# Forgetting attention and a bilinear feed-forward on one core: reciprocals of the softmax sums as powers on GpSimd, from the third batch on

## The chip, the cores and the metric

The kernel runs on one core of a Trainium2 chip. The metric is the device time of one execution in microseconds (us); lower is better. Engines go by the names of the profile: PE (TensorE matmuls), PEld (its weight loads), DVE (VectorE), ACT (ScalarE), POOL (GpSimd), SP (SyncE, which here only issues DMAs).

## The reference

Attention with a forget gate, over 8 batches, 8 heads, 576 positions and a head size of 64, is followed by a bilinear feed-forward over the 4608 tokens of 512 features:

```python
scores = scale * np.matmul(q, k.transpose(0, 1, 3, 2))
cum = np.cumsum(np.log(np.clip(f, 0.0001, 1.0)), axis=-1)
scores = np.where(causal, -1e9, scores + cum[:, :, :, None] - cum[:, :, None, :])
attn = np.exp(scores - np.max(scores, axis=-1, keepdims=True))
attn = attn / (np.sum(attn, axis=-1, keepdims=True) + 1e-09)
x = np.matmul(attn, v)                  # then heads side by side: 4608 x 512
out = ((x @ w_a) * (x @ w_b)) @ w_out   # d_ff = 1536
```

The division by the row's sum is what the change is about.

## The kernel before

The unit of attention is a pair of heads of one batch, numbered t from 0 to 31 (four pairs a batch). Its 576 query rows are five blocks i: four of 128 rows, for which both heads are worked on one after the other, and a last one, i = 4, with 64 rows of each head side by side on the 128 partitions. For each block, in this order:

- PE multiplies q and k into PSUM (`qk_first`, `qk_group`; tiles sc). From the third batch on a POOL copy (`last_queries`, L610, tile qd) first lays out the last 64 queries.
- DVE adds the decay from the tile spread to the scores, writes them to S, and takes the row's maximum in the same instruction (`do_decay`, L673, one for each head). In the first batch a plain maximum is taken instead (L645). The causal mask lies in spread; POOL makes it there (`mask_copy`, L630, and `mask_last`, L637).
- ACT takes the exponential into the tile PA (blocks 0 to 2) or PB (blocks 3 and 4) and sums the rows as it goes (`do_exp`, L700 and L704). In the profile each shows as an ACTIVATE and an ACTIVATION_READ_ACCUMULATOR, which writes the sum.
- DVE takes the reciprocal of the sums (`do_recip`, L712 for block 4 with one column, L714 for the others with two columns, one for each head).
- POOL multiplies PA or PB by the reciprocals (`do_norm`, L725, one instruction for each head). In the first two batches ACT may do some of these (L723); from the third batch on POOL does all.
- A DMA from SP transposes PA and PB into PTA and PTB (`do_tr`, L739), PE multiplies these by v (`do_pv_all`, L768 and L783, tile pvx), and ACT or DVE copies the result to xT.

The maxima, sums and reciprocals of a head pair lie in one small tile st of 128 x 32 values: sums from column 10 (18 for block 4), reciprocals from column 20 (28 for block 4).

POOL has other work in between: it converts q, k and v to 16 bit (L290, L292), and issues some loads. The feed-forward runs beside the attention of later batches: PE's products psa and psb (all in L74), a copy of psa by ACT (L288), the product ht by DVE (L1072), PE's pso, and a copy and a store. The last 1024 tokens go through a scheme with fewer products (wg, wb), where POOL and DVE combine tiles in L1273.

Nothing is scheduled when the program is built: every step is an `Op` with a number, the list ORDER gives all 2463 numbers in one sequence, and each step is emitted to its engine as the sequence comes to it. So an engine's queue is that sequence with the other engines' steps left out. CHOICE gives the engine of those steps that have more than one. Each engine works through its queue strictly in turn; waits on other engines are semaphores that the framework puts in.

`EARLY` is (0, 1), the first two batches; `NP`, the head pairs of a batch, is 4.

Of the kernel before, what the change touches and what calls it, by code (L numbers as in the profile page):

```python
# [9 lines left out]
FP32 = mybir.dt.float32  # L10
# [15 lines left out]
def kernel(  # L26
# [11 lines left out]
    nc = tc.nc  # L38
# [7 lines left out]
    NP = H // 2  # L46
# [3 lines left out]
    def pool(name, bufs=1, **kw):  # L50
        return ctx.enter_context(tc.tile_pool(name=name, bufs=bufs, **kw))

    perm = pool("perm")
# [18 lines left out]
    def mm_halves(out, lhsT, rhs, **kw):  # L72
        for r in HP:
            nc.tensor.matmul(out=out[r], lhsT=lhsT[:, r], rhs=rhs, **kw)  # L74

    def identity():
        make_identity(nc, ident16)

    def wake(n):
        x = ff_tile([128, 512], FP32, "wake")  # L80
        for _ in range(n):
            mm_halves(x, ident16, ident16[:, 0:1].to_broadcast([128, 512]), start=True, stop=True, skip_group_check=True)
# [22 lines left out]
    def paddings():  # L105
        for x in (*qd, lowd):
            nc.gpsimd.memset(x, 0.0)
        for r in HP:
            nc.gpsimd.tensor_copy(out=lowd[r, r], in_=low[0][r, 0:64])
        for x in PB:  # L110
            nc.gpsimd.memset(x[:, 12, 64:128], 0.0)
        for i in range(2):
            nc.gpsimd.memset(nv[i][64:128, NSB - 1, :, :], 0.0)

# [74 lines left out]
    def take(op, tag):  # L189

        users = [op]
        op.takes.append((tag, users))
        return users
# [53 lines left out]
    for n in range(24):  # L247
        o = Op("PE", 0.427, lambda _: wake(2), [o_i], prio=-290, mode="full", name=f"wake{n}")
# [7 lines left out]
    for lo, hi in ((0, 256), (256, S)):  # L256
# [3 lines left out]
            out=cw["l"][FR, lo:hi], in_=cw["f"][FR, lo:hi], func=LN), [o1, o_w], prio=-300, name="fln")  # L260
        o3 = Op("DVE", 0.02 + 0.00232 * n, lambda _, lo=lo, hi=hi: scan(lo, hi), [o2, o0] + ([o3] if lo else []),
                prio=-300, name="fscan")
        o4 = Op("DVE", 0.06 + 0.0007 * n, lambda _, lo=lo, hi=hi: nc.vector.tensor_copy(
            out=crow[FR, lo:hi], in_=cw["f"][FR, lo:hi]), [o3], prio=-300, name="fhi")
# [8 lines left out]
    for u in s_users:  # L273
        u.extend([o_f[1], o6])
    o_p = Op("POOL", 4.0, lambda _: paddings(), [o_c], prio=-100)


# [106 lines left out]
    EARLY = tuple(range(2))  # L384
# [255 lines left out]
    def do_max(t, i):  # L640
        if ("st", t) not in T:
            T[("st", t)] = slot(st_pool, [128, 32], FP32, "st", "st")
        st = T[("st", t)]
        m = st[:, 8:9] if i == 4 else st[:, 2 * i:2 * i + 2]
        nc.vector.tensor_reduce(out=m, in_=T[("s", t, i)], axis=AXX, op=MAX, negate=True)  # L645
# [31 lines left out]
    def part_of(t, i):  # L677

        if i >= 3:
            return "B"  # L680
        return ("A0" if i < 2 else "A1") if t // NP in EARLY else "A"
# [26 lines left out]

    def do_recip(t, i):
        st = T[("st", t)]  # L710
        if i == 4:
            nc.vector.reciprocal(out=st[:, 28:29], in_=st[:, 18:19])  # L712
        else:
            nc.vector.reciprocal(out=st[:, 20 + 2 * i:22 + 2 * i], in_=st[:, 10 + 2 * i:12 + 2 * i])  # L714

    def do_norm(e, t, i, h):
        st = T[("st", t)]
        if i == 4:
            p, c = p_blocks(t, 4), 28
        else:  # L720
            p, c = p_blocks(t, i)[:, :, h, :], 20 + 2 * i + h
        if e == "ACT":
            nc.scalar.activation(out=p, in_=p, func=COPY, scale=st[:, c:c + 1])  # L723
            return
        VEC[e].tensor_scalar(out=p, in0=p, scalar1=st[:, c:c + 1], scalar2=1.0, op0=MUL, op1=MUL)  # L725
# [87 lines left out]
    def in_turn(o, kind, n, started=False):  # L813

        if (kind, n) not in first_of:
            first_of[(kind, n)] = o
            p = first_of.get((kind, n - 1))
            if p is not None:
                (o.prev if started else o.deps).append(p)

    def attention(t, base):
        b, pr = divmod(t, NP)

        def prio(g):
            if b == 0:
                return -100 + (3.0 * pr if g == 0 else 20 + 8 * pr + g)
            if b in EARLY:
                return base - 10 * pr + (3.0 * pr if g == 0 else 12 + 7 * pr + g)
            return base + g
# [30 lines left out]
        for gs in ([(0,), (1,), (2, 3)] if b in EARLY else [(0, 1), (2,), (3,)]):  # L860
# [5 lines left out]
            def stage(_, gs=gs):  # L866
# [3 lines left out]
                for g in gs:  # L870
# [3 lines left out]
                    prio=prio(gs[0]), mode="full" if full else "row", name=f"qk{t}.{gs[0]}")  # L874
            if full:
                cp = Op("POOL", 0.4, lambda _: last_queries(t), [kq_ops[("q", b, pr)], o_p] + last_qd[-1:], prio=prio(0),
                        name=f"qd{t}")
# [20 lines left out]
        for g, gi in [(g, groups[g]) for g in ((0, 1, 3, 2) if t in MASKP else (0, 1, 2, 3))]:  # L898
            qk, su = qk_of[g], None
            for i in gi:  # L900
                sc = users_of[i]
                part = part_of(t, i)
                mxs = []
                for h in range(1 if direct else 2):
                    fn = (lambda _, i=i: do_max(t, i)) if direct else lambda _, g=g, i=i, h=h: do_decay(t, g, i, h)
                    mx = Op("DVE", (MAXD if direct else RED)[i], fn,
                            [qk] if direct else [qk, bcs[h] if t not in MASKP or i == 4 else ml if i == 3 else mc], prio=prio(g),
                            name=f"max{t}.{i}")
                    if t in MASKP and i == 4:
                        ml.deps.append(mx)  # L910
                    in_turn(mx, "max" + part[0], t)
                    if st_users is None:
                        st_users = take(mx, "st")
                    else:
                        mx.deps.append(st_users[0])
                        st_users.append(mx)
                    if direct:
                        su = sc
                    else:
                        if su is None:  # L920
                            su = take(mx, "S")
                        else:
                            mx.deps.append(su[0])
                            su.append(mx)
                        bcu.append(mx)
                    (sc[h] if isinstance(sc, tuple) else sc).append(mx)
                    mxs.append(mx)
                    if direct:
                        for x in direct_ex.get(g, []):
                            x.deps.append(mx)  # L930
                es = []
                for h in range(1 if i == 4 else 2):
                    ex = Op("ACT", EXPD[i], lambda _, i=i, h=h: do_exp(t, i, h),
                            mxs if i == 4 or direct else mxs[h:h + 1], prio=prio(g),
                            name=f"exp{t}.{i}")
                    if direct:
                        ex.deps.append(o_e)
                        direct_ex.setdefault(g, []).append(ex)
                    ex.tail = 0.005
                    in_turn(ex, "exp" + part[0], t)  # L940
                    if part not in pu:
                        if part == "A1":
                            ex.deps.append(pu["A0"][0])
                            pu["A0"].append(ex)
                            pu[part] = pu["A0"]
                        else:
                            pu[part] = take(ex, "P" + part[0])
                        if part == "B":
                            ex.deps.extend([o_p] + last_pb[-1:])
                            last_pb.append(ex)  # L950
                    else:
                        ex.deps.append(pu[part][0])
                        pu[part].append(ex)
                    es.append(ex)
                su.extend(es)
                rc = Op("DVE", 0.16, lambda _, i=i: do_recip(t, i), es, prio=prio(g))
                st_users.extend(es + [rc])
                for h in range(1 if i == 4 else 2):
                    nm = Op(None, {"POOL": NORM[i]} | ({"ACT": 0.2 + 0.00082 * 128 * (i + 1)} if b in EARLY else {}), lambda e, i=i, h=h: do_norm(e, t, i, h), [rc], prio=prio(g),
                            name=f"norm{t}.{i}")  # L960
                    st_users.append(nm)
                    pu[part].append(nm)
                    norms.setdefault(part, []).append(nm)
                    norm_of.append((i, nm))
        trs, ptu = {}, {}
        la_users = None
        for part in norms:
            lo, hi = BLOCKS[part]
            p = prio({"A0": 0, "A1": 1}.get(part, 2))
            if b in PEP or (t, part) in PEQ:  # L970
                cuts = {"A": [(0, 6), (6, 12)], "A0": [(0, 6)], "A1": [(6, 12)], "B": [(0, 8), (8, 13)]}[part]
                trs[part] = []
                for lo, hi in cuts:
# [7 lines left out]
                            prio=p - 0.5, name=f"pev{t}{part}")  # L981
# [46 lines left out]
        for rows in [(0, 1), (2, 3)]:  # L1028
# [5 lines left out]
                    prio=p, mode="col", name=f"pv{t}")  # L1034
            pvu = take(pv, "ff")
            ev = Op("DVE", 0.15 + 0.00106 * 128 * len(rows), lambda e, rows=rows: do_ev(e, t, rows), [pv], prio=p - 1,
                    name=f"ev{t}")
# [319 lines left out]
    for b in range(B):  # L1357
        batch_inputs(b, 40.0 * b + (-100.0 if b == 0 else 0.0))
        if b == 0:
            weights(-85.0)  # L1360
        for pr in range(NP):
            attention(b * NP + pr, 40.0 * b + 10.0 * pr + 30)
# [168 lines left out]
```

## Time and profile before

| | |
|---|---|
| median of 2 runs (lowest to highest) | 396.73 us (396.17 to 397.29) |
| the profiled execution, its own time | 395.96 us |
| its span, first to last instruction | 393.9 us |
| busy: PE, DVE, ACT, POOL | 382.3, 319.2, 296.5, 280.4 us |
| L725 on POOL, scaling of PA (180) and of PB (90) | 85.6 and 64.0 us |
| L673 on DVE, decay and maximum, the form with 232 | 125.4 us |
| L704 on ACT, exponential, PA (168) and PB (56) | 84.1 and 40.2 us |

In the profile's groups a row reads: line, engine, operation, the tile written and those read with their shapes, the count; then busy time in all and the mean ns of one; then how long the engine stood idle just before such instructions, and which engine's instruction ended most of that. In the timeline a row is: start, length, engine, line, operation, tiles; an x2 at its end says that two like instructions were merged, and brackets give the idle time ahead with what ended it. A group of waits reads: who waited, for whom, us in all, how often, and the longest. All times are from the start of the span.

### The profile page before, as it was taken

Reading aid. Unit: us, or ns where it says so; the run is one execution under the profiler, and the core shown is the slowest. Engines: PE = TensorE matmul, PEld = TensorE weight load, DVE = VectorE, ACT = ScalarE, POOL = GpSimd, SP = SyncE. Lnnn points to the kernel's source line nnn. Section 1 sums busy time; section 2 is a strip of 40 time slices with the busy share of each in tenths; the row PEclk is TensorE's granted clock in tenths of the full one; section 3 lists DMA queues with packets and bytes.
Section 4 is the critical chain, followed back from the end, with each engine's and each line's share of the span. In section 5 each row is a group of like instructions: output and inputs, shape, how many; then the busy total and the mean of one; then the engine's idle time right before and its main releaser. Section 6 shows DMA issues by size and latency. Waiting matters only on the chain.

```text
span 393.9 us, 14686 instructions
## 1 busy us (share of the span) xinstructions
PE 382.3 (97%) x5720; PEld 251.3 (64%) x5720; DVE 319.2 (81%) x1015; ACT 296.5 (75%) x817; POOL 280.4 (71%) x482
## 2 busy tenths in 40 slices
PE   7899999999999999999999999999999989999997
PEld 3557977969766665655555665555655677666665
DVE  7888898998997779788887798758998898989700
ACT  4998999999888878778988588789898662455221
POOL 8699677778877689884897779678976980357600
PEclk9999999999999999999999999999999999999999
DMA  7999999999999999999999999999999895100022
GB/s 125 265 188 173 153 147 232 231 289 284 188 233 245 219 285 211 263 236 266 256 229 264 256 227 213 260 270 229 207 203 223 185 139 137 55 1 2 2 108 107
DMA packets 147365, 76.87 MB, mean 195 GB/s; under 512 B 124384, under 2 KB 128352, under 8 KB 147296
## 3 DMA queue, kind: packets, MB, share of 16 engines
q1 hardware_dynamic: 132856, 68.72, 77.2%
q0 software_dynamic: 14256, 7.08, 14.6%
q8 instruction: 44, 0.72, 0.7%
q14 instruction: 25, 0.20, 0.2%
q10 hardware_dynamic: 184, 0.14, 0.1%
HBM read 52.05 MB, written 9.58 MB: 156 GB/s over the span
## 4 chain that ended last, share of the span: by engine, by line
PE 79%; DMA 7%; POOL 4%; DVE 4%; ACT 3%; issue 2%; DVEq 0%; ACTq 0%; POOLq 0%
PE pso L74 20%; PE psa L74 16%; PE psb L74 15%; PE wg L74 5%; PE wb L74 4%; PE sc L550 3%; PE pvx L768 3%; DMA PTB<-PB 2%; PE psT L358 2%; DMA wout<-in_moe_w_out_dram 2%; POOL PA L725 2%; PE sc L538 2%; ACT PA L704 2%; PE wake L74 2%; DVE S L673 2%
## 5 line engine op out<-in xcount | busy, mean ns | idle before, releaser
L673 DVE CUSTOM_DVE_ANT_0 S<-sc,spread 64x576 f32<-64x576 f32 (+4 forms) x232 | 125.4, 561 | 14.2 <-ACT PA L704 4.8
L725 POOL TENSOR_SCALAR PA<-PA,st 128x256 f16<-128x256 f16 (+2 forms) x180 | 85.6, 487 | 10.5 <-DVE st L714 7.5
L74 PE MATMUL psa<-xT,wa 128*64 128x512 f16 (+2 forms) x864 | 88.9, 333 | 1.7 <-DVE ht L1072 1.7
L74 PE MATMUL psb<-xT,wb 128*64 128x512 f16 (+2 forms) x864 | 88.7, 332 | 0.4 <-DVE ht L1072 0.2
L704 ACT ACTIVATE PA<-S,st 128x256 f16<-128x256 f32 (+2 forms) x168 | 84.1, 503 | 6.2 <-DVE st L673 5.7
L74 PE MATMUL pso<-wout,ht 128*64 128x512 f16 x696 | 85.5, 380 | 0.3 <-DMA wout<-in_moe_w_out_dram 0.3
L725 POOL TENSOR_SCALAR PB<-PB,st 128x512 f16<-128x512 f16 (+1 forms) x90 | 64.0, 719 | 23.4 <-DVE st L714 8.7
L74 PEld LDWEIGHTS <-wa 128*64 128x64 f16 x960 | 55.4, 110 | 26.3 <-issue 4.2
L74 PEld LDWEIGHTS <-wb 128*64 128x64 f16 x960 | 56.5, 110 | 24.3 <-issue 1.7
L288 ACT CAST a<-psa 128x512 f16<-128x512 f32 (+1 forms) x90 | 49.4, 551 | 18.1 <-PE psa L74 14.9
L1072 DVE TENSOR_TENSOR ht<-psb,a 128x512 f16<-128x512 f32 (+1 forms) x90 | 57.6, 649 | 6.2 <-PE psb L74 4.1
L74 PEld LDWEIGHTS <-ht 128*64 128x64 f16 x696 | 38.8, 110 | 27.9 <-issue 2.6
L704 ACT ACTIVATE PB<-S,st 128x512 f16<-128x512 f32 x56 | 40.2, 720 | 3.4 <-DVE st L673 2.9
L704 ACT ACTIVATION_READ_ACCUMULATOR PA<-S,st 128x1 f32 x168 | 31.9, 190 | 0.0
L700 ACT ACTIVATE PB<-S,st 128x576 f16<-128x576 f32 x28 | 21.7, 776 | 9.2 <-DMA PTB<-PB 3.6
L630 POOL TENSOR_SCALAR_AFFINE_SELECT spread<-spread 128x768 f32<-128x768 f32 x24 | 20.9, 871 | 10.7 <-DMA spread<-cum_d 10.3
L288 ACT COPY osb<-pso 128x512 f32<-128x512 f32 x28 | 16.3, 583 | 15.4 <-PE pso L74 15.4
L768 PEld LDWEIGHTS <-nv 128*64 128x64 f16 x640 | 22.0, 110 | 6.7 <-DMA PTA<-PA 2.1
L1273 POOL TENSOR_TENSOR hy<-wu 128x512 f16<-128x512 f32 x9 | 11.4, 1278 | 20.3 <-DVE wu L1273 20.3
L673 DVE CUSTOM_DVE_ANT_1 S<-sc,spread 128x256 f32<-128x256 f32 x48 | 19.7, 420 | 6.5 <-PE sc L538 1.9
L714 DVE RECIPROCAL st<-st 128x2 f32<-128x2 f32 x128 | 18.2, 156 | 7.4 <-ACT PA L704 3.8
L673 DVE DVE_READ_ACCUMULATOR2_ANT st<- 128x1 f32 (+1 forms) x280 | 22.9, 82 | 0.0
(136 smaller groups left out, 674.6 us busy)
## 6 DMA issues: line engine op xcount, KB each, us to landing
spread<-cum_d SPq DMA_DIRECT2D x24, 576.0 KB, 6.4
out_dram<-osb SPq DMA_DIRECT2D x35, 256.0 KB, 3.4
q<-in_q_dram SPq DMA_DIRECT2D x14, 576.0 KB, 5.3
k<-in_k_dram SPq DMA_DIRECT2D x14, 576.0 KB, 5.1
v<-in_v_dram SPq DMA_DIRECT2D x24, 256.0 KB, 6.0
wout<-in_moe_w_out_dram POOLq DMA_DIRECT2D x3, 512.0 KB, 8.0
nv<-in_v_dram POOLq DMA_DIRECT2D x8, 128.0 KB, 5.9
wa<-in_moe_w_a_dram POOLq DMA_DIRECT2D x2, 512.0 KB, 7.6
```

The lines of the kernel that those rows point to most:

```text
L74: nc.tensor.matmul(out=out[r], lhsT=lhsT[:, r], rhs=rhs, **kw)
L288: nc.scalar.copy(out=out_, in_=in_)
L550: nc.tensor.matmul(out=dst, lhsT=lhsT, rhs=rhs, start=start, stop=stop, skip_group_check=True)
L630: nc.gpsimd.affine_select(out=c[:, :, 0:SM].rearrange("p h (j k) -> p h j k", k=128), in_=c[:, :, SM:2 * SM].rearrange("p h (j k) -> p h j ...
L673: nc.vector.tensor_tensor_reduce(out=o, in0=x, in1=y, scale=-1.0, scalar=3e38, op0=ADD, op1=MIN, accum_out=m)
L700: nc.scalar.activation(out=p_blocks(t, 4), in_=T[("s" if direct else "z", t, 4)], func=EXP, bias=st[:, 8:9], scale=sign, accum_out=st[:, 1 ...
L704: nc.scalar.activation(out=p_blocks(t, i)[:, :, h, :], in_=(T[("s", t, i)][:, h, :] if direct else T[("z", t, i)][:, h * n:h * n + n]).rea ...
L714: nc.vector.reciprocal(out=st[:, 20 + 2 * i:22 + 2 * i], in_=st[:, 10 + 2 * i:12 + 2 * i])
L725: VEC[e].tensor_scalar(out=p, in0=p, scalar1=st[:, c:c + 1], scalar2=1.0, op0=MUL, op1=MUL)
L768: nc.tensor.matmul(out=o[HP[h], 128 * i:128 * i + 128], lhsT=vt[:, j, pr + NP * h, :], rhs=pt[:, base_blk[i] + 2 * block_at(t, i, j) + h, ...
L1072: nc.vector.tensor_tensor(out=ht[:, 0:n_], in0=T.pop(("psb", t0, fbs))[:, 0:n_], in1=T.pop(("a16", t0, fbs))[:, 0:n_], op=MUL)
L1273: VEC[e].tensor_tensor(out=out_, in0=x, in1=y, op=op)
```

## The change

For the head pairs of the third batch on (t from 8 to 31), the reciprocal becomes a two-operand power on POOL, of the sums and of a tile of -1.0, in the place of DVE's reciprocal. The first two batches keep theirs. The tile, minus, has two columns and is filled by POOL at the start. The step keeps its number and so its place in ORDER; the `Op` now names POOL, and has the start's POOL step `o_p` (in which minus is filled) among those that it follows.

```diff
+    minus = perm.tile([128, 2], FP32, tag="minus", name="minus")
...
+        nc.gpsimd.memset(minus, -1.0)
...
     def do_recip(t, i):
         st = T[("st", t)]
-        if i == 4:
-            nc.vector.reciprocal(out=st[:, 28:29], in_=st[:, 18:19])
+        o, x = (st[:, 28:29], st[:, 18:19]) if i == 4 else (st[:, 20 + 2 * i:22 + 2 * i], st[:, 10 + 2 * i:12 + 2 * i])
+        if t // NP in EARLY:
+            nc.vector.reciprocal(out=o, in_=x)
         else:
-            nc.vector.reciprocal(out=st[:, 20 + 2 * i:22 + 2 * i], in_=st[:, 10 + 2 * i:12 + 2 * i])
+            nc.gpsimd.tensor_tensor(out=o, in0=x, in1=minus[:, 0:1 if i == 4 else 2], op=mybir.AluOpType.pow)
...
-                rc = Op("DVE", 0.16, lambda _, i=i: do_recip(t, i), es, prio=prio(g))
+                rc = Op("DVE" if b in EARLY else "POOL", 0.16, lambda _, i=i: do_recip(t, i), es if b in EARLY else [*es, o_p], prio=prio(g))
```

The queues of PE, ACT and SP hold the same instructions in the same order as before. DVE's loses 120 reciprocals, POOL's gains 120 powers and the memset. Three places of POOL's queue show where the powers come to stand. Rows give line, operation, tile written and tiles read, and the shape; lines from do_recip on are four higher in the changed kernel (L718 is the power, L729 the scaling that was L725), and the numbers of tiles two higher (st_5410 and st_5412 are the same tile; PB0_82 is now PB0_83).

The first place, some 212 to 221 us into the trace of before. Before, on POOL:

```order
L630 AFFINE_SELECT spread0_84<-spread0_84 128x2x384
L292 CAST k16_5565<-k32_5544 128x2x9x64
L725 TENSOR_SCALAR PA_5186<-PA_5186,st_5162 128x2x128
L725 TENSOR_SCALAR PA_5186<-PA_5186,st_5162 128x3x128
L725 TENSOR_SCALAR PB1_83<-PB1_83,st_5162 128x4x128 x2
L725 TENSOR_SCALAR PA_5186<-PA_5186,st_5162 128x3x128
L725 TENSOR_SCALAR PA_5418<-PA_5418,st_5410 128x2x128
L290 TENSOR_SCALAR q16_5749<-q32_5547 128x2x9x64
```

And now:

```order
L633 AFFINE_SELECT spread0_85<-spread0_85 128x2x384
L295 CAST k16_5567<-k32_5546 128x2x9x64
L718 TENSOR_TENSOR st_5164<-st_5164,minus_72 128x1
L718 TENSOR_TENSOR st_5164<-st_5164,minus_72 128x2 x2
L718 TENSOR_TENSOR st_5412<-st_5412,minus_72 128x2
L718 TENSOR_TENSOR st_5412<-st_5412,minus_72 128x1
L729 TENSOR_SCALAR PA_5188<-PA_5188,st_5164 128x2x128
L729 TENSOR_SCALAR PA_5188<-PA_5188,st_5164 128x3x128
L729 TENSOR_SCALAR PB1_84<-PB1_84,st_5164 128x4x128 x2
L729 TENSOR_SCALAR PA_5188<-PA_5188,st_5164 128x3x128
L729 TENSOR_SCALAR PA_5420<-PA_5420,st_5412 128x2x128
L293 TENSOR_SCALAR q16_5751<-q32_5549 128x2x9x64
```

Five powers now stand between the conversion of k and the scalings of the head pair of st_5164; the last of them belongs to block 4 of the next head pair, st_5412.

The second place, about 257 to 261 us. Before, on POOL:

```order
L725 TENSOR_SCALAR PA_6140<-PA_6140,st_6131 128x128
L725 TENSOR_SCALAR PA_6427<-PA_6427,st_6420 128x2x128
L637 AFFINE_SELECT spread0_84<-spread0_84 128x2x128
L610 COPY qd0_63<-qT_5789 64x64 x2
L725 TENSOR_SCALAR PB1_83<-PB1_83,st_6131 128x4x128
L725 TENSOR_SCALAR PB1_83<-PB1_83,st_6131 128x576
```

And now:

```order
L718 TENSOR_TENSOR st_6422<-st_6422,minus_72 128x2
L729 TENSOR_SCALAR PA_6142<-PA_6142,st_6133 128x128
L729 TENSOR_SCALAR PA_6429<-PA_6429,st_6422 128x2x128
L640 AFFINE_SELECT spread0_85<-spread0_85 128x2x128
L718 TENSOR_TENSOR st_6422<-st_6422,minus_72 128x1
L718 TENSOR_TENSOR st_6671<-st_6671,minus_72 128x2
L613 COPY qd0_63<-qT_5791 64x64 x2
L729 TENSOR_SCALAR PB1_84<-PB1_84,st_6133 128x4x128
L729 TENSOR_SCALAR PB1_84<-PB1_84,st_6133 128x576
```

The copies into qd0, and what follows them, now stand behind a power of the head pair st_6671.

The third place, the end of the attention, about 319 to 321 us. Before, on POOL:

```order
L725 TENSOR_SCALAR PA_7494<-PA_7494,st_7467 128x128
L725 TENSOR_SCALAR PA_7494<-PA_7494,st_7467 128x3x128
L725 TENSOR_SCALAR PB0_82<-PB0_82,st_7604 128x576
L725 TENSOR_SCALAR PA_7612<-PA_7612,st_7604 128x3x128
L725 TENSOR_SCALAR PA_7612<-PA_7612,st_7604 128x128
```

And now:

```order
L729 TENSOR_SCALAR PA_7496<-PA_7496,st_7469 128x128
L729 TENSOR_SCALAR PA_7496<-PA_7496,st_7469 128x3x128
L729 TENSOR_SCALAR PB0_83<-PB0_83,st_7606 128x576
L718 TENSOR_TENSOR st_7606<-st_7606,minus_72 128x2
L729 TENSOR_SCALAR PA_7614<-PA_7614,st_7606 128x3x128
L729 TENSOR_SCALAR PA_7614<-PA_7614,st_7606 128x128
```

A power of the last head pair, for its block 3, has come ahead of the last scalings of PA.

## The prediction

> **What bounds the kernel now.** The page comes first, for the span, the engines' shares and the slices:
>
> ```profile
> span 393.9 us, 14686 instructions
> PE 382.3 (97%) x5720; PEld 251.3 (64%) x5720; DVE 319.2 (81%) x1015; ACT 296.5 (75%) x817; POOL 280.4 (71%) x482
> PE   7899999999999999999999999999999989999997
> POOL 8699677778877689884897779678976980357600
> PEclk9999999999999999999999999999999999999999
> ```
>
> PE is at work in 97% of the span at the full granted clock. Its queue runs attention and feed-forward matmuls interleaved in a written order, so what enters PE's queue as a wait is added to the time: PE has 393.9 - 382.3 = 11.6 us of idle to win back, and no spare work to put into a new hole. POOL is not the bound, but it is far from free. I read it next in the stretch in which the changed instructions stand:
>
> ```profile
> 82.00:326.00 244.00, 240.40 (x3506) 150.45 (x3504) 205.68 (x729) 198.47 (x569) 193.30 (x349) 1.00 1.08 235
> ```
>
> The columns are PE, PEld, DVE, ACT and POOL. In these 244 us PE is idle for 3.6 and POOL for 244 - 193.3 = 50.7. Third, the groups of instructions and the waits:
>
> ```profile
> L714 DVE RECIPROCAL st<-st 128x2 f32<-128x2 f32 x128 | 18.2, 156 | 7.4 <-ACT PA L704 3.8
> L712 DVE RECIPROCAL st<-st x32: 142/154/165, 34.5 to 318.8; 128x1 f32<-128x1 f32 x32
> POOL PB L725 <- DVE st L714: 8.7, 6, 2.7
> POOL PA L725 <- DVE st L714: 7.5, 6, 2.4
> ```
>
> A reciprocal costs DVE 0.155 us, and ahead of the L714 group DVE stood idle for 7.4 us in all, for an exponential on ACT. POOL waited for L714 12 times, 16.2 us. These waits are what the change can remove; PE does not stand behind most of them.
>
> **What the change removes.** Of 128 + 32 reciprocals, the 8 head pairs of the first two batches keep 5 each; 160 - 40 = 120 leave DVE: 120 x 0.155 = 18.6 us of its busy time, and the idle time ahead of some. POOL's scaling instructions no longer wait for DVE. I carried these savings down the queues alone (the method is below), with powers that take no time and wait for nothing on POOL: the end comes 0.7 us earlier. So the removal is worth at most 0.7 us, since DVE bounds nothing in the stretch and PE's 3.6 us of holes there have other causes. The new memset of the constant is one short instruction at the start; at 0.1 us (the row with 99 ns below) and hidden by PE's first work, it counts nothing, or 0.1 without that cover.
>
> **What it adds: a wait at the head of POOL's queue.** The order of the program is kept, so each power takes the place in POOL's queue that its position in the order gives, ahead of scalings that on POOL ran long before that exponential was done. On DVE the same wait held up DVE alone. To price this I took each power in the changed order, the end of the exponential that it waits for, and the start of POOL's next instruction, both from the trace of before. Of 120 powers 75 carry a wait for ACT; in 32 of those the exponential ends after POOL had already gone on, by 53.8 us summed, 7.25 at most. The largest, in rows of POOL, ACT, DVE and PE:
>
> ```profile
> 214.30 1.04 POOL L725 TENSOR_SCALAR PA<-PA,st 128x256 f16<-128x256 f16 x2
> 217.32 1.36 POOL L725 TENSOR_SCALAR PB<-PB,st 128x512 f16<-128x512 f16 x2 [1.98 <-issue]
> 219.66 1.16 POOL L290 TENSOR_SCALAR q<-q 128x1152 f16<-128x1152 f32 x1
> 221.36 0.19 ACT L700 ACTIVATION_READ_ACCUMULATOR PB<-S,st 128x1 f32 x1
> 221.58 0.17 DVE L712 RECIPROCAL st<-st 128x1 f32<-128x1 f32 x1 [0.98 <-ACT PB L700]
> 222.46 0.33 PE L358 MATMUL psT<-ident,q 64*128 64x64 f16 x3
> ```
>
> DVE took this reciprocal at 221.58, right after ACT's sum at 221.36 + 0.19 = 221.55. In the new queue it stands ahead of the scalings that POOL began at 214.30: POOL waits 221.55 - 214.30 = 7.25 us, and behind it stand the scalings of another head pair and the conversion of q. Of the 7.25 the idle 1.98 us at 217.32 swallows its own length. The conversion ended at 220.82 and PE's transpose took q at 222.46: 1.64 us, less about 0.2 for handing over and loading weights (my estimate). PE is late by 7.25 - 1.98 - 1.44 = 3.8 us. The second place:
>
> ```profile
> 260.47 0.53 POOL L610 COPY qd<-qT 64x64 f16<-64x64 f16 x2
> 265.20 1.14 POOL L292 CAST k<-k 128x1152 f16<-128x1152 f32 x1 [0.52 <-DMA k<-in_k_dram]
> 266.65 0.87 POOL L630 TENSOR_SCALAR_AFFINE_SELECT spread<-spread 128x768 f32<-128x768 f32 x1
> 265.27 0.20 ACT L704 ACTIVATION_READ_ACCUMULATOR PA<-S,st 128x1 f32 x1
> 268.69 0.42 DVE L673 CUSTOM_DVE_ANT_1 S<-sc,spread 128x256 f32<-128x256 f32 x1 [0.32 <-PE sc L538]
> 269.60 0.60 PE L74 MATMUL psa<-xT,wa 128*64 128x512 f16 x4
> ```
>
> The power ahead of the q copies at 260.47 waits for ACT until 265.47: 5.0 us. Idle swallows 0.5; the mask copy ended at 267.52 and DVE's decay used it at 268.69, 1.2 us of slack; that decay frees a PSUM bank at 269.1 and PE writes there at 269.60, 0.4 of slack after some handing over. PE is late by 5.0 - 0.5 - 1.2 - 0.4 = 2.9. The last place:
>
> ```profile
> 320.24 1.50 POOL L725 TENSOR_SCALAR PA<-PA,st 128x384 f16<-128x384 f16 x3
> 323.18 0.19 ACT L704 ACTIVATION_READ_ACCUMULATOR PB<-S,st 128x1 f32 x1
> 323.83 4.20 SPq L739 DMA_TRANSPOSE PTB<-PB  x2
> 329.91 0.25 PE L768 MATMUL pvx<-PTB,nv 128*64 128x128 f16 x2
> ```
>
> Here POOL would wait 323.37 - 320.24 = 3.1 us ahead of the last scalings, whose transposes PE takes up as soon as they land; about 3.0 reach PE, with no work left to hide them.
>
> The whole stage is counted in the same way, with two running numbers: how late POOL is against before, and how late PE is. A power sets POOL's lag to at least PE's lag plus its own overshoot; idle of POOL that another engine ended lets the lag shrink; PE's lag grows to POOL's less the slack of what PE takes. All other durations, DMA times included, stay as traced. With a power of no length PE's lag grows by 1.1 at 102 us, 1.5 at 120, 3.0 from 150 to 162, 1.2 at 186, 0.4 at 204, 3.8 at 222, 0.3 at 261, 3.1 at 269, 2.0 from 274 to 277, 0.5 at 304 and 3.0 at 330: 19.9, which with small steps is **20.0 us**.
>
> **What it adds: the power's own length.** No power stands in the trace. The nearest rows of POOL, and one of DVE:
>
> ```profile
> L725 POOL TENSOR_SCALAR PA<-PA,st 128x256 f16<-128x256 f16 x60 | 29.0, 490 | 0.7
> L725 POOL TENSOR_SCALAR PA<-PA,st 128x128 f16<-128x128 f16 x58 | 21.6, 375 | 6.5 <-DVE st L714 4.3 <-issue 1.9
> L1273 POOL TENSOR_TENSOR hy<-wu 128x512 f16<-128x512 f32 x9 | 11.4, 1278 | 20.3 <-DVE wu L1273 20.3
> L1515 POOL MEMSET const-float32-1.0<- 128x1 f32 x1 | 0.1, 99 | 0.0
> L1273 DVE TENSOR_TENSOR wu<-wb,wu 128x512 f32<-128x512 f32 x24 | 16.3, 686 | 2.9 <-ACT wv L288 0.7 <-PE wb L74 0.6 <-ACT wu L288 0.5
> ```
>
> Below, 0.10: the shortest instruction of POOL. Above, 1.28: the two-operand product over 512 columns, which a power of two columns reaches only if each is worth 256 products. Two scalings differ by 115 ns for 128 columns, so an empty one costs 375 - 115 = 260 ns. I take **0.35 us**, that floor and a third for the power, nearer to the small instructions because two columns are little work. The count with this length gives 33.3 us, so the length adds 13.3 to the 20.0: 120 x 0.35 = 42 us of POOL's work, of which much runs in the 50.7 us of idle. At 0.10 the sum is 22.8, at 0.6 50, at 0.8 68, at 1.0 88, at 1.28 119: beyond 50.7 / 120 = 0.42 us POOL is full and each further 0.1 costs 7 to 12.
>
> [...]
>
> **Sum.** -0.7 is within the count, so +33.3 us against the profiled execution's 395.96 (393.9 of span and 2.1 around it): 429.3. The median of the runs shown is 396.73, 0.8 more; against it the time is **430.0 us**.
>
> **Rivals.** First, the other side: **the waits move from DVE to POOL without reaching PE**, not slower. The mechanism is that POOL's 50.7 us of idle and the slack ahead of PE take in every overshoot, while DVE is free of its own. For it: 43 of 75 waits find the exponential done, and POOL lost 16.2 us to DVE that it now keeps. Against it: the three places above, where I find slack of 1 to 4 us against 3 to 7. It decides where the overshoots shrink below that slack; then with a power of 0.1 to 0.16 us the sum is -0.7 to +0.2, a time of 396 to 397. Second, **the power is long and POOL becomes the bound**, from 0.6 us on. For it: a power is a longer computation than any in the rows of POOL. Against it: two columns. Time: 396.7 + 50 to 119, 447 to 516, and past 1.28 us beyond. Third, **a power as short as a memset**, so that only the wait at the queue's head remains: 396.7 + 20 to 23, 417 to 420; it lies at the low end of the forecast and is counted with it.
>
> **How the numbers follow.** The forecast with 0.1 to 0.6 us a power, whose own range is 413 to 447 (the low end takes a third off the 20 us, since my count lets no DMA arrive sooner), has a chance of 0.67; the long power 0.27; the other side 0.06. The range 413 to 515 runs from that low end to the price of 1.28 us; outside it lie the other side and part of the long powers, under 2 in 10. Faster by over 2% (about what a measurement of this kernel tells from no change, 8 us): 0.02. Within 2%: 0.04, the other side's most. Slower: 0.94.
>
> **What would show it.** POOL's row for L718 with 120 instructions near 0.35 us; idle on POOL ahead of L718 released by ACT, some 36 us summed, with one wait near 5 us around 238; PE waits for POOL's q and k and for DMA of PTA and PTB, which hardly exist now; PE busy as before in a span near 427; DVE's reciprocals down to 40. It is wrong if PE's idle stays near 11.6 us in spite of idle ahead of L718 (then slack was larger than I read), if L718 never waits, or if a power takes over 0.6 us, in which case POOL's slices read 9 from the eighth to the thirty-third and the time is far above.

## The result, and the profile after

The changed kernel takes 453.22 us (median of 2 runs, 452.11 to 454.33) against 396.73: a ratio of 1.142, 95% interval 1.137 to 1.147. It is 56.5 us slower. The time lies in the stated range, 413 to 515, but above the forecast's own range of 413 to 447: it is the second rival, the long power, that came.

The page of the profile after, span, shares and slices:

```profile
span 450.4 us, 14679 instructions
PE 399.6 (89%) x5720; PEld 258.1 (57%) x5720; DVE 309.7 (69%) x895; ACT 297.1 (66%) x817; POOL 360.1 (80%) x603
PE   7899999997979886899979699996788986899997
POOL 8698757699998987987997999968999988056610
PEclk9999999998999987999989899996999999799999
```

The same work of PE now lies in a span 56.5 us longer. POOL's busy time went up by 79.7 us, ACT's stayed, DVE's fell by 9.5: less than the 18.6 us of reciprocals taken away, since these partly overlap their neighbours on DVE (three in a row took 0.28 us in the trace of before; the decay kept its length, 564 against 561 ns). PEclk is no longer full everywhere.

The added instructions, from the groups of POOL by form:

```profile
L718 POOL TENSOR_TENSOR st<-st,minus 128x2 f32<-128x2 f32 x96 | 65.6, 697 | 20.7 <-ACT PA L707 13.8 <-ACT PB L707 6.4 <-PE sc L74 0.3
L718 POOL TENSOR_TENSOR st<-st,minus 128x1 f32<-128x1 f32 x24 | 13.3, 558 | 3.0 <-DMA out_dram<-osb 2.9
```

A power of two columns takes 697 ns and one of one column 558, on average 0.67 us where the prediction took 0.35. Ahead of them POOL stood idle for 23.7 us, most of it for ACT's exponentials. The two longest waits of one engine for another, and then PE's own three longest:

```profile
DVE S L676 <- POOL spread L640: 35.6, 15, 5.1
ACT PB L707 <- DVE st L676: 25.2, 14, 4.2
...
PE psT L361 <- POOL q L293: 8.7, 3, 4.1
PE pvx L772 <- DVE st L676: 6.4, 4, 2.2
PE pvx L772 <- DMA PTB<-PB: 5.1, 2, 4.5
```

DVE waits for POOL's mask (35.6 us, where that wait stood at 2.1 us before), ACT for DVE, and PE for what POOL converts (q), for decays that free its banks, and for the transposes of what POOL scales. The stretch of the attention, with the same columns as in the prediction:

```profile
82.00:382.00 300.00, 259.15 (x3532) 158.82 (x3527) 199.84 (x614) 198.77 (x567) 272.85 (x469) 0.95 0.83 192
```

It is 300 us long in place of 244. POOL is busy for 272.85 of them, 91%. The first place of the prediction looks like this on POOL, with ACT's sum:

```profile
240.12 0.87 POOL L633 TENSOR_SCALAR_AFFINE_SELECT spread<-spread 128x768 f32<-128x768 f32 x1
240.95 1.13 POOL L295 CAST k<-k 128x1152 f16<-128x1152 f32 x1
242.06 2.52 POOL L718 TENSOR_TENSOR st<-st,minus 128x1 f32<-128x1 f32 x4
247.20 0.19 ACT L703 ACTIVATION_READ_ACCUMULATOR PB<-S,st 128x1 f32 x1
247.46 0.55 POOL L718 TENSOR_TENSOR st<-st,minus 128x1 f32<-128x1 f32 x1 [2.88 <-DMA out_dram<-osb]
```

Between the conversion of k and the scalings stand five powers: 2.52 us for four, an idle 2.88 us, and the fifth. The page names a DMA as what ended the idle time, but of what this instruction reads only ACT's sum was late, and that ended at 247.20 + 0.19 = 247.39. The 7.25 us of wait that the trace of before promised have become 2.88: POOL is 30.3 us later here than before (244.58 against 214.30), the sum only 25.8 (247.39 against 221.55).

What came of it on PE, at the first place and at the third:

```profile
251.36 1.16 POOL L293 TENSOR_SCALAR q<-q 128x1152 f16<-128x1152 f32 x1
252.57 0.66 PE L361 MATMUL psT<-ident,q 64*128 64x64 f16 x18 [4.11 <-POOL q L293]
373.14 0.72 POOL L718 TENSOR_TENSOR st<-st,minus 128x2 f32<-128x2 f32 x1
383.71 0.32 PE L772 MATMUL pvx<-PTB,nv 128*64 128x128 f16 x2 [4.55 <-DMA PTB<-PB]
```

At both PE stood idle as foreseen, for q (4.11 us) and for PTB (4.55). But at the third the power itself waited for nothing, and POOL had no idle from 370.48 on: there the lag that POOL had gathered came through to PE, and not that power's own wait.

### The profile page after: what moved, and what is told of

Its sections match the earlier page's. It is cut to its first block, busy times and chain, and to the rows that moved or that the text cites. A ratio compares the mean times of both kernels' runs of the same rounds, so it can differ in the third digit from the quotient of the medians.

```text
span 450.4 us, 14679 instructions
## 1 busy us (share of the span) xinstructions
PE 399.6 (89%) x5720; PEld 258.1 (57%) x5720; DVE 309.7 (69%) x895; ACT 297.1 (66%) x817; POOL 360.1 (80%) x603
## 5 line engine op out<-in xcount | busy, mean ns | idle before, releaser
L676 DVE CUSTOM_DVE_ANT_0 S<-sc,spread 64x576 f32<-64x576 f32 (+4 forms) x232 | 125.2, 564 | 59.4 <-POOL spread L640 35.6
L74 PE MATMUL psa<-xT,wa 128*64 128x512 f16 (+2 forms) x864 | 95.7, 349 | 8.4 <-DVE st L676 4.6
L718 POOL TENSOR_TENSOR st<-st,minus 128x2 f32<-128x2 f32 (+1 forms) x120 | 78.4, 669 | 23.7 <-ACT PA L707 13.8
L74 PE MATMUL psb<-xT,wb 128*64 128x512 f16 (+2 forms) x864 | 92.8, 341 | 4.2 <-DVE st L676 4.1
L74 PE MATMUL pso<-wout,ht 128*64 128x512 f16 x696 | 88.5, 389 | 2.6 <-DVE st L676 2.6
L729 POOL TENSOR_SCALAR PA<-PA,st 128x256 f16<-128x256 f16 (+2 forms) x180 | 86.7, 492 | 4.6 <-DVE st L716 3.6
L74 PEld LDWEIGHTS <-wa 128*64 128x64 f16 x960 | 57.7, 113 | 36.3 <-issue 15.7
L74 PEld LDWEIGHTS <-wb 128*64 128x64 f16 x960 | 58.6, 113 | 30.9 <-issue 9.9
L729 POOL TENSOR_SCALAR PB<-PB,st 128x512 f16<-128x512 f16 (+1 forms) x90 | 66.5, 745 | 6.0 <-DVE st L716 4.7
L772 PEld LDWEIGHTS <-nv 128*64 128x64 f16 x640 | 23.6, 114 | 17.6 <-issue 11.9
L1277 POOL TENSOR_TENSOR hy<-wu 128x512 f16<-128x512 f32 x9 | 11.5, 1281 | 20.4 <-DVE wu L1277 20.4
L772 PE MATMUL pvx<-PTA,nv 128*64 128x128 f16 x288 | 16.4, 228 | 6.4 <-DVE st L676 6.4
```

The costliest lines, as they stand in the source:

```text
L676: nc.vector.tensor_tensor_reduce(out=o, in0=x, in1=y, scale=-1.0, scalar=3e38, op0=ADD, op1=MIN, accum_out=m)
L718: nc.gpsimd.tensor_tensor(out=o, in0=x, in1=minus[:, 0:1 if i == 4 else 2], op=mybir.AluOpType.pow)
L772: nc.tensor.matmul(out=o[HP[h], 128 * i:128 * i + 128], lhsT=vt[:, j, pr + NP * h, :], rhs=pt[:, base_blk[i] + 2 * block_at(t, i, j) + h, ...
L1277: VEC[e].tensor_tensor(out=out_, in0=x, in1=y, op=op)
```

## The experiments

**The length and the place, one at a time.** The first runs put the two parts of the loss into a square: power or short product, in its place or just ahead of its first scaling. The product has the power's operands and waits; where it stands, rows are scaled by minus their sum.

```diff
# e1_product_in_place
-            nc.gpsimd.tensor_tensor(..., op=mybir.AluOpType.pow)
+            nc.gpsimd.tensor_tensor(..., op=MUL)
```

> The power is replaced by a product of the same operands at the same place of POOL's queue (the scalings then use minus the sum, so the output is another). It keeps each wait for ACT and changes only the instruction's length, which POOL's short rows put at 0.2 to 0.3 us against 0.70 and 0.56 for the power. Theory A, waits at the head of POOL's queue cost 20 us by themselves and length comes on top: 423 to 428 us. Theory B, the length alone makes the loss and the waits are taken in by POOL's idle: 400 to 407 us.

Measured: 424.55 us, ratio 1.070 (1.062 to 1.077). The groups of POOL:

```profile
L718 POOL TENSOR_TENSOR st<-st,minus 128x2 f32<-128x2 f32 x96 | 17.4, 195 | 35.0 <-ACT PA L707 20.1 <-ACT PB L707 12.6 <-PE sc L74 2.1
L718 POOL TENSOR_TENSOR st<-st,minus 128x1 f32<-128x1 f32 x24 | 4.5, 191 | 7.5 <-ACT PB L703 7.4
```

The product takes 0.19 us, and still the kernel loses 27 us: 22 us of work went to POOL, and 42.5 us of idle stand ahead of it, 40.1 of them for ACT. Theory B is out for a short instruction.

```diff
# e2_power_late (in laid_out; late_rc holds each power with its scalings)
+        for rc, nms in late_rc.items():
+            seq.remove(rc)
+            seq.insert(min(seq.index(nm) for nm in nms), rc)
```

> Each power is moved in the order to just ahead of the first scaling that uses it; nothing else changes. That takes away the waits at the head of POOL's queue and keeps 120 powers of full length. Sum of parts as the prediction made it (20 us of waits and the rest length): 453 - 20 = 433 us. Theory C, the two do not add, because once POOL is full its lag makes most exponentials done before POOL comes to them: by the count with measured lengths 397 + 51 = 448 us, and idle ahead of the power under 1 us in place of 23.7.

> Both edits: product in place of the power, and just ahead of its first scaling (the output is another). With no wait ahead of other work and a short instruction little is left. By the count with 0.2 to 0.3 us: 403 to 411 us. If moving an instruction from DVE to POOL cost something of its own that neither wait nor length explains, it would stay above 415 us; if the work on DVE was what held the kernel, it would fall under 396.

The third run has both edits. Measured: late powers 453.05 us (1.142, 1.135 to 1.150), late products 406.62 (1.022, 1.010 to 1.033). With the short instruction the place is worth 424.55 - 406.62 = 18 us or more, as the late products bring a wait of their own (told next); with the long one nothing at all, and the sum of parts, 433, is wrong by 20. Theory C had 448; the waits for ACT went, as it said, but 5 us more stayed. POOL's groups with late powers:

```profile
L719 POOL TENSOR_TENSOR st<-st,minus 128x2 f32<-128x2 f32 x96 | 68.4, 713 | 0.6
L730 POOL TENSOR_SCALAR PB<-PB,st 128x512 f16<-128x512 f16 x61 | 44.0, 726 | 6.3 <-DVE st L717 3.7
L730 POOL TENSOR_SCALAR PA<-PA,st 128x384 f16<-128x384 f16 x62 | 36.2, 587 | 4.0 <-DVE st L717 1.5
L730 POOL TENSOR_SCALAR PA<-PA,st 128x256 f16<-128x256 f16 x60 | 29.1, 490 | 2.6
L730 POOL TENSOR_SCALAR PB<-PB,st 128x576 f16<-128x576 f16 x29 | 21.7, 748 | 3.5 <-DVE st L717 1.1
L730 POOL TENSOR_SCALAR PA<-PA,st 128x128 f16<-128x128 f16 x58 | 21.5, 374 | 5.1 <-DVE st L717 2.5
```

Ahead of the powers no idle time is left, but ahead of the scalings there are 6.3 + 4.0 + 2.6 + 3.5 + 5.1 = 21.5 us, where the changed kernel has 4.4 + 1.9 + 0.3 + 1.6 + 2.4 = 10.6. A scaling right behind its power waits until that is done. (The late products have it too: 21.1 us ahead of the five groups, against 11.5 for products in place.) The last run of the study tells whether this took the place of the waits:

```diff
# e13_power_one_ahead: as late powers, but one POOL instruction earlier,
# not ahead of the exponentials that the power needs
-            seq.insert(min(seq.index(nm) for nm in nms), rc)
+            at = min(seq.index(nm) for nm in nms)
+            first = 1 + max(seq.index(d) for d in rc.deps)
+            while at > first and (seq[at - 1].eng != "POOL" or seq[at - 1] in late_rc):
+                at -= 1
+            seq.insert(max(at - 1, first), rc)
```

> Late powers again, but each one POOL instruction earlier, where its exponentials stand ahead of that, so that most scalings no longer follow directly on their power. With late powers, POOL's idle ahead of the scalings is 21.5 us against 10.6 in the changed kernel: a scaling directly behind its power waits for the power to be done. If that handing over took the place of the waits for ACT, the time falls to 397 + 42 = 439 us, and idle ahead of the scalings to some 12 us. If the place has no effect at all once POOL is full, it stays at 453 us.

Measured: 440.56 us (1.109, 1.102 to 1.116). The groups:

```profile
L719 POOL TENSOR_TENSOR st<-st,minus 128x2 f32<-128x2 f32 x96 | 67.5, 704 | 3.0 <-ACT PB L708 1.9
L730 POOL TENSOR_SCALAR PB<-PB,st 128x512 f16<-128x512 f16 x61 | 43.9, 723 | 4.1 <-DVE st L717 3.7
L730 POOL TENSOR_SCALAR PA<-PA,st 128x128 f16<-128x128 f16 x58 | 21.4, 372 | 2.7 <-DVE st L717 2.6
```

The five groups of scalings have 4.1 + 1.6 + 0.3 + 1.5 + 2.7 = 10.2 us of idle again, and the time falls by 12.5 us. So late powers had exchanged one wait for another. With the power, waits are worth 453.22 - 440.56 = 12.7 us, not nothing.

**The length alone.** DVE takes all reciprocals again; POOL does a power of the constant at each place.

```diff
# e6_power_no_wait
+    spare = perm.tile([128, 2], FP32, tag="spare", name="spare")
...
+        nc.gpsimd.tensor_tensor(out=spare[:, 0:n], in0=minus[:, 0:n], in1=minus[:, 0:n], op=mybir.AluOpType.pow)
```

> All reciprocals are back on DVE as before. At the same 120 places of POOL's queue stands a power of the constant tile into a spare tile, which waits for nothing and which nobody reads. It is the length alone, at the places of the change. Theory C (POOL is full with 120 powers, waits add little): by the count with 0.70 and 0.56 us, 397 + 42 = 439 us. Theory A (20 us of waits plus the rest): 453 - 20 = 433 us at most, and if half the loss were from DVE's lost reciprocals or from how the scalings wait, under 425 us. It also shows whether the power's length depends on its operands: 697 ns for two columns again, or not.

Measured: 440.45 us (1.108, 1.103 to 1.114).

```profile
L722 POOL TENSOR_TENSOR spare<-minus 128x2 f32<-128x2 f32 x96 | 66.7, 694 | 4.1
...
82.00:370.00 288.00, 255.54 (x3550) 157.55 (x3549) 208.34 (x736) 199.63 (x569) 273.56 (x470) 0.98 0.90 201
```

The first row is a group, the second the stretch, 288 us of which POOL works 273.56. The length alone costs 440.45 - 397.74 = 42.7 us (against the kernel before on the same chip). A power is as long with other operands, 694 ns. And the time equals that of the run just told, 440.56, in which DVE has 120 reciprocals less: these two show no gain from taking them off DVE. They differ in the place of the powers as well, so a small gain could hide behind a small loss.

**The number.** The 32 reciprocals that the prediction had found too early on POOL go back to DVE.

```diff
# e4_32_back_on_dve
+    BACK = {(8, 0), (8, 3), (9, 0), (9, 1), (10, 0), (10, 1), (10, 4), ...}   # 32 pairs (t, i)
-                rc = Op("DVE" if b in EARLY else "POOL", ...
+                rc = Op("DVE" if b in EARLY or (t, i) in BACK else "POOL", ...
```

> The 32 reciprocals whose exponential ended, in the trace of before, after POOL had gone on are taken by DVE again; the other 88 stay powers on POOL in their place. Theory of length alone: the loss shrinks with the number, 88/120 of 56.5 us, 438 us. Theory of waits and length: the waits go as well, and the count gives 397 + 25 = 422 us.

Measured: 417.29 us (1.052, 1.045 to 1.060), 5 us better than the count and 21 better than by numbers alone. A quarter of the powers, chosen by their waits in the trace of before, carries 36 of the 56 us. The group of two-column powers and the attention's stretch:

```profile
L719 POOL TENSOR_TENSOR st<-st,minus 128x2 f32<-128x2 f32 x68 | 46.5, 695 | 8.2 <-ACT PA L708 8.0
82.00:347.00 265.00, 244.65 (x3488) 151.35 (x3484) 197.21 (x636) 197.76 (x567) 248.81 (x437) 0.99 0.96 216
```

The 32 held most of the waiting: ahead of the powers 8.2 + 0.8 = 9.0 us of idle are left of 23.7. POOL is busy for 94% of this shorter stretch, so it is as full as with 120 powers; it has less to do and waits less.

**POOL's total work.** The scalings from the third batch on are cut to 64 columns (the other columns stay unscaled), in the kernel with late powers, in the changed kernel and in the kernel before.

```diff
# e8_power_late_short_scalings, e9_power_in_place_short_scalings, e10_before_short_scalings
+        if t // NP not in EARLY:
+            p = p[:, 0:64] if i == 4 else p[:, 0, 0:64]
         VEC[e].tensor_scalar(out=p, in0=p, scalar1=st[:, c:c + 1], ...)
```

> As the run with late powers, but from the third batch on each scaling works on 64 columns only (the other columns stay unscaled, so the output is another). That takes 216 x 0.2 to 0.45 us, some 55 us, of work from POOL and leaves every wait and every instruction in place. If POOL's total work is the cause (theory C), most of the 56 us comes back: by the count 397 + 9 = 406 us. [...]

> The changed kernel, powers in their place, with the same short scalings (output another). POOL is no longer behind, so by theory C it comes early to the powers again and the waits at the head of its queue cost what they cost with the short product: by the count 397 + 24 = 421 us, 15 more than with late powers. If the waits never cost anything, it equals the run with late powers.

> The kernel before with the same short scalings (output another), the base for the two others: is POOL's work a bound of the kernel before? By the count 397 - 0.5, no change. If POOL bounded it, the time would fall by over 5 us.

Measured: 406.64 us (1.022, 1.015 to 1.029) with late powers, 417.99 (1.050, 1.043 to 1.057) with powers in place, and 392.72 (0.989, 0.984 to 0.994) for the kernel before. In the second one the waits are back:

```profile
L718 POOL TENSOR_TENSOR st<-st,minus 128x2 f32<-128x2 f32 x96 | 66.0, 698 | 28.3 <-ACT PA L707 17.6 <-ACT PB L707 10.0
L718 POOL TENSOR_TENSOR st<-st,minus 128x1 f32<-128x1 f32 x24 | 13.2, 553 | 6.4 <-ACT PB L703 6.3
```

The powers are as long as ever, but with some 50 us of other work gone 46 of the 56 us come back with late powers. A POOL that is less behind reaches the powers in place before ACT has finished: 34.7 us of idle in place of 23.7. The third run missed its expectation of no change: with 51 us less work on POOL the kernel before gains 5 us, 1.1%, a small amount but with an interval clear of 1. POOL's work does hold it up a little.

**Towards a faster kernel.** From that I tried the kernel before with less on POOL: its 24 scalings of block 4 from the third batch on by DVE, and by ACT, in the same places.

```diff
# e11_before_block4_on_dve (e12_before_block4_on_act has "ACT")
-                    nm = Op(None, {"POOL": NORM[i]} | (...), ...
+                    nm = Op(None, {"DVE": 0.4} if b not in EARLY and i == 4 else {"POOL": NORM[i]} | (...), ...
```

> The kernel before, with one edit towards less work on POOL: from the third batch on the 24 scalings of block 4 (128x576, 0.75 us each on POOL) are done by DVE at the same place of the order. The run with short scalings took some 55 us from POOL and gained 5 us, so 24 x 0.75 = 18 us taken away should gain 1 to 2 us if DVE takes them without delay: 395 to 397 us. If DVE's queue is delayed by them, 400 us or more.

> The same 24 scalings on ACT (0.74 us each in the first two batches) in place of POOL. ACT then waits in its queue for the reciprocal on DVE, at a place where POOL used to come late. If POOL's work is what bounds a little: 395 to 397 us. If ACT's queue, which feeds the exponentials, is held up: 400 us or more.

Measured: 405.53 us (1.019, 1.015 to 1.024) and 402.35 (1.014, 1.010 to 1.017). Both are slower, by little but with intervals clear of 1, although DVE does such a scaling in 423 ns:

```profile
L725 DVE TENSOR_SCALAR PB<-PB,st 128x576 f16<-128x576 f16 x24 | 9.9, 423 | 0.2
```

The idle ahead of it is only 0.2 us, so a wait at its own head does not explain the 8.6 us. What PE met is in the trace: it waited 4.4 us for PTA and 3.2 for PTB, where before it waited 1.1 for PTA; and POOL waited 21.2 us for DVE's L714 where it had 16.2. That points to a delay of DVE's queue, the case that the expectation put at 400 us or more, but which instruction starts it was not settled. No run of this study that computes the full result beats the kernel before.

**The power by its width.** As the length alone, with 1, 2, 4, 8 and 16 columns (both constant tiles get 16).

```diff
# e7_power_widths
-        n = 1 if i == 4 else 2
+        n = (2, 4, 8, 16, 1)[i]
```

> As the run of powers that wait for nothing, with the power's width set by the block: 2, 4, 8, 16 columns for blocks 0 to 3 and 1 for block 4. It measures the power's length by its width. From 697 ns for two columns and 558 for one, a straight line gives 419 + 139 ns a column: 975 ns for 4, 1531 for 8, 2643 for 16. If POOL worked 16 values at a time along a row, all widths would take about 560 to 700 ns. The total is of no interest; a straight line makes it about 0.7 + 0.98 + 1.53 + 2.64 + 0.56 = 6.4 us for each of 24 head pairs, so over 480 us.

Measured: 518.44 us in one run. The groups:

```profile
L722 POOL TENSOR_TENSOR spare<-minus 128x16 f32<-128x16 f32 x24 | 69.6, 2901 | 1.2
L722 POOL TENSOR_TENSOR spare<-minus 128x8 f32<-128x8 f32 x24 | 39.4, 1640 | 1.0
L722 POOL TENSOR_TENSOR spare<-minus 128x4 f32<-128x4 f32 x24 | 24.3, 1011 | 0.9
L722 POOL TENSOR_TENSOR spare<-minus 128x2 f32<-128x2 f32 x24 | 16.8, 700 | 0.9
L722 POOL TENSOR_TENSOR spare<-minus 128x1 f32<-128x1 f32 x24 | 13.4, 557 | 1.0
```

The length grows by 143 to 158 ns a column, on some 400 ns that every power pays; from four columns on that is 4 to 10% above the straight line of the expectation. The product of the same shape takes 195 ns for two columns and 191 for one.

## Why the prediction came out as it did

- **What bounds the kernel**: right. PE had no spare work for new holes, and all of the loss lies in the stretch of the attention, 300 us in place of 244.
- **The removal, worth at most 0.7 us**: right. With the power's length on POOL and few waits, DVE with its reciprocals (440.45) and without them (440.56) make the same time, and late products, with DVE relieved, were no faster than the kernel before.
- **A wait at the head of POOL's queue, 20.0 us**: right as a mechanism, and in size for a short instruction: the product in place is 18 us slower than the late one, and the prediction's sums of 22.8 at 0.10 us and 33.3 at 0.35 put a product of 0.19 at 26.6 on a straight line, where 27.0 was measured. With the power the size was not right (12.7, below). The 0.2 us that the first place took for handing q over and loading weights was an estimate that no row shows: in the changed kernel PE's weight load and its transpose both began 0.05 us behind the conversion (252.57 against 251.36 + 1.16). PE's waits came for q, for PTB and for banks; those for k and PTA did not.
- **The power's own length, 0.35 us**: this term failed. It measured 0.70 and 0.56 us, 0.67 on average. The floor of POOL's short instructions was not too low (the product takes 0.19, the prediction read 0.26), but by the widths a power costs some 0.21 us on top for being a power (the 0.40 that every power pays, less the product's 0.19) and about 0.15 for each column. The step "two columns are little work" was the wrong one: a column costs a power (143 to 158 ns) about what a whole reciprocal costs DVE (156). The prediction's own sums of 50 at 0.6 us and 68 at 0.8 give 56 at 0.67, and 56.5 was measured: the input failed and not the method. That it fits to half a microsecond is partly luck, since the count knows nothing of PE's clock (last section) and missed the late powers by 5 us.
- **The sum, 20.0 for waits and 13.3 for length**: the split is the other way round. The length alone is 42.7 us, and the waits add 12.7, not 20, to make 453.2: a POOL that is behind finds more exponentials done. The idle ahead of L718 is 23.7 us, where the prediction had 36 for its shorter power.
- **Against the instruction it replaces**: two columns took 697 ns as a power on POOL and 156 as a reciprocal on DVE, a factor of 4.5. No run here has a power on DVE, so this does not compare one operation on both engines. No single power stands out: the longest of the 120 is 735 ns, and the first began 0.08 us behind the ACT sum that it waited for (84.27 against 84.00 + 0.19), after 3.30 us of idle.
- **The rivals**: the long power had 0.27 against 0.67 for the forecast, and it came, with 447 to 516 stated. That the time lies in the stated range is owed to this rival's price and not to the forecast's own term. What spoke for it, that a power is a longer computation than any in POOL's rows, was the better reading (697 ns against 195 for a product of the same shape). The other side, no loss, was never near: even the cheapest form tried here, a 0.19 us product just ahead of its use, lost 2.2% (1.0 to 3.3).
- **The signs named ahead**: DVE's reciprocals fell to 40, and POOL waited ahead of L718 for ACT. But PE's busy time rose by 17.3 us where it was to stay as before, and POOL's slices from the eighth to the thirty-third read 6 to 9, where a long power was to make all of them 9.

## What to carry to other kernels

An instruction that is moved to another engine in a fixed order brings along its wait: look up in the trace what that engine had already done when the awaited result came, and add up what will now stand behind it. Such waits and the instruction's length do not add: here the waits shrank on an engine that became full, and came back when load was taken from it (idle ahead of L718: 42.5 us with the short product, 23.7 with the power, 34.7 with the power and short scalings). Price an operation that no row of the trace shows by measuring it, by itself and at two widths, before its place in the queue is discussed; here it was 2.9 to 3.6 times as long as a product of the same shape.

## What the runs showed of the hardware

In the changed kernel PE's granted clock fell to 0.50 seven times up to the last matmul, each time in one of its longer holes or up to 0.41 us behind it. A hole of 3.03 us, which ended when POOL's conversion of q came, and what followed it:

```profile
104.93 0.44 PE L361 MATMUL psT<-ident,q 64*128 64x64 f16 x18 [3.03 <-POOL q L293]
105.30 1.49 PE L74 MATMUL psa<-xT,wa 128*64 128x384 f16 x8
111.87 0.82 PE L74 MATMUL psa<-xT,wa 128*64 128x384 f16 x8
...
101.00:104.90 3.90, 0.91 (x14) 0.41 (x8) 2.50 (x9) 1.53 (x6) 3.90 (x8) 1.00 0.56 120
105.33:108.74 3.41, 3.41 (x26) 1.70 (x24) 1.24 (x3) 1.86 (x5) 3.41 (x6) 0.50 1.05 219
109.00:113.00 4.00, 4.00 (x70) 2.55 (x68) 2.61 (x9) 2.23 (x7) 3.84 (x10) 1.00 1.03 268
```

The last column but two is the granted clock: 1.00 in the hole, 0.50 for the 3.41 us behind it, then 1.00 again. Eight products for psa took 1.49 us at the half clock and 0.82 later. In this trace the seven longest holes between two matmuls, 2.66 to 4.55 us, each went with 3.4 or 6.8 us at half the clock; holes of 2.04 and 2.24 us did not. The length of a hole alone did not decide it: in the run with late powers and short scalings, one of 3.48 us left the clock at 1.00.

```profile
343.34 0.25 PE L775 MATMUL pvx<-PTB,nv 128*64 128x128 f16 x2 [3.48 <-DMA PTB<-PB]
343.35:347.00 3.65, 3.65 (x54) 2.60 (x55) 2.14 (x6) 1.36 (x3) 0.00 (x0) 1.00 0.00 0
```

The mean clock was 0.962 in the changed kernel and 1.000 with late products. Over 450.4 us the missing 0.038 is worth 17.1 us of PE at full speed, and PE's busy time did grow by 399.6 - 382.3 = 17.3 us for the same matmuls. How much of the 56.5 us that is stays open. The count of lags knows no clock and still comes to 56, so much of the slower time of PE may lie where PE would have waited anyway, but no run held the clock up to show it. The split into length and waits is not free of it either: PE was busy for 395.0 us with powers that wait for nothing, 393.1 with powers one ahead and 400.1 with late powers, so up to 7.0 of the 12.5 us between the last two can be the clock that fell after the waits.
